# Sixteen loads of the experts' first weights: issued by GpSimd in place of SyncE

## The chip, the cores and the metric

The kernel runs on one core of a Trainium2 chip. The metric is the device time of one launch in microseconds (us), as the median of several runs. A profiled execution gives the trace: which instruction ran on which engine and when, and when each DMA was issued and landed. The engines are TensorE (PE; its weight loads are shown as PEld), VectorE (DVE), ScalarE (ACT), GpSimd (POOL) and SyncE (SP), which here does nothing but issue DMAs. The DMAs of a core run on 16 DMA engines.

## The reference

Three stages follow each other: a causal attention with a window of 64 positions, a soft mixture of experts, and a feed-forward layer with a sigmoid-approximated GELU. All arrays are float32.

```
scores = q @ k.T / sqrt(64), masked to 0 <= i - j < 64    # B, H, S, D = 4, 8, 576, 64
x = softmax(scores) @ v                                   # laid out as 2304 tokens x 512
logits = x @ phi                                          # 512 x 32: 8 experts, 4 slots each
slot_in = softmax over tokens(logits).T @ x
for e in range(8):
    slot_out[e] = relu(slot_in[e] @ w1[e]) @ w2[e]        # w1[e] 512 x 1024, w2[e] 1024 x 512
x = softmax over slots(logits) @ slot_out
h = x @ w_in                                              # 512 x 2048
out = (h * sigmoid(1.702 * h)) @ w_out                    # 2048 x 512
```

w1 and w2 are 16.8 MB each, the largest inputs by far. On the host both are cut into 16 slices of 1 MiB, `[128, 2048]` float32, so that a slice is one DMA with 8 KB for each of the 128 partitions.

## The kernel before

The kernel is one long program with an order written out by hand (`manual_schedule`). Three stages can be told apart in time.

**Attention, with routing in between.** A loop over `i` in 0 to 17 (lines 613 to 672) works on 16 units (a batch and a pair of heads) and two tails. In iteration `i` TensorE computes the scores of unit `i` (`emit_s`, the mask product at L313 and the products at L328), transposes the weights of unit `i - 1` (L348) and multiplies them by v (`emit_pv`, L363). GpSimd prepares what TensorE reads: `scale_q` of the next unit (L236), after that unit's q and k have landed; `set_ones` (L244) and `shift_v` (L248, L251) of this unit, after its v has landed. Every second iteration it also limits a slice of the feed-forward weights that is converted early (`narrow_c`, L161). These are plain Pool instructions, in program order.

SP's order within an iteration is: `load_qk` three units ahead (L226; L228 for the tails), `load_v` two units ahead (L240), and `load_w` (L146), which takes the next slices from the list `plan`: first the 16 of w1, then the 16 of w2. Iterations 2 to 11, 13 and 14 load one slice, 15 and 16 two each, 17 three (`W_AT`, line 35; iteration 12 loads none). For `i` in `AHEAD` (10 to 15) the slice stands between `load_qk` and `load_v`. So w1 is exhausted after iteration 16, and all later calls of `load_w` load w2. `load_qk` waits for its ring of three buffers (the scores of unit `i` have been computed), and `load_v` for its own (the products with v of unit `i - 1`). The slots of w1 are new memory, but for the last three, which held early raw weights.

The first seven slices of w2 go into memory of the attention stage (`dslot`), and are issued as that comes free near the end of the loop and in the tail after it (L691, L720, L745). The last nine go into slots of w1, and are issued as the products with w1 (L792) have read them.

**Experts.** TensorE multiplies by w1 (L792), the result is transposed (`emit_ht`), and it multiplies by w2 (L834; the last slice, in three pieces, at L901).

**Feed-forward.** From there to the end TensorE runs the feed-forward products (L1014, L1046) while SP loads the rest of w_in and w_out.

The line that is changed is in `load_w`:

```
for c in PIECES if not plan else (slice(0, 4),):
    nc.sync.dma_start(out=t[:, c], in_=v[:, c])
```

Of the kernel before, what the change touches and what calls it, by code (L numbers as in the profile page):

```python
# [69 lines left out]
def attention_softmoe_ffn(  # L70
# [12 lines left out]
    nc = tc.nc  # L83
# [41 lines left out]
    def wslot(dtype=F32):  # L125
        return wp.tile([128, 4, 512], dtype, tag="w", name="w")

    def dslot(i):
        return mem(2048 * i, 2048).rearrange("p (a f) -> p a f", a=4)
# [6 lines left out]
    def load_w(n=1):  # L136
        for _ in range(n):
            if plan:
                lst, src, i, d = plan.pop()
                t = wslot() if d is None else dslot(d)  # L140
                v = src[i].rearrange("p (a f) -> p a f", a=4)
                if not plan:
                    t, v = [x.rearrange("p a f -> p (a f)").rearrange(
                        "p (c a f) -> p c a f", c=4, a=4) for x in (t, v)]
                for c in PIECES if not plan else (slice(0, 4),):
                    nc.sync.dma_start(out=t[:, c], in_=v[:, c])  # L146
                lst.append(t)


# [463 lines left out]
    for i in range(ns):  # L613
# [49 lines left out]
        if i in AHEAD:  # L663
            load_w(W_AT.get(i, 0))
# [6 lines left out]
        if i not in AHEAD:  # L671
            load_w(W_AT.get(i, 0))
# [10 lines left out]
        out=ml[:, 128:160], in_=pm[0:1, 0:128].rearrange("p (t s) -> p s t", t=TM), axis=AX.X,  # L683
# [5 lines left out]
    emit_pv(ns - 1)  # L689
    emit_norm(ns - 1)  # L690
    load_w(1)  # L691

    lpt = bank("s")[:, 0:256]
    mm = sp.tile([128, 3], F32, tag="mm", name="mm")

    def tail_logits(t):
# [11 lines left out]
        out=mm[:, 2:3], in0=pm[:, 0:1], scalar1=-1.0, scalar2=None, op0=ALU.mult)  # L708
# [15 lines left out]
        out=ltt, in_=lpt, func=ACTF.Exp, bias=m, scale=1.0, accum_out=ss)  # L724
# [14 lines left out]
    for c in range(2):  # L739
# [9 lines left out]
        out=rsl, in0=pm[:, 0:1], scalar1=ss, scalar2=1e-9, op0=ALU.add, op1=ALU.add)  # L749
# [3 lines left out]
        out=i4s, in0=i4m[:, 0:NS], scalar1=rsl, scalar2=None, op0=ALU.mult)  # L753
    nc.vector.scalar_tensor_tensor(
        out=acc, in0=psl, scalar=al, in1=acc, op0=ALU.mult, op1=ALU.add)
# [479 lines left out]
```

## Time and profile before

| | us |
|---|---|
| runs before, median of 3 | 364.0 (362.63 to 367.21) |
| the profiled execution's own time | 362.31 |
| its span, first to last instruction | 360.5 |
| around the span | 1.8 |

A row of the page's second part cuts the span into 40 slices of 9.0 us, and a digit is the busy share in tenths. In a timeline a row is: start, duration, engine, line, operation, what it writes and reads, and in brackets how long the engine was idle before and what ended that. `SPq` and `POOLq` are the sequencers. An issue of a DMA by SP is short; its landing is told separately. In the chain of waits each row is start, duration and what held the program up. The names: `w` are the slots of 1 MiB, `arena` and `rawt` memory of the attention stage, `in_w_dram` both w1 and w2 in HBM, `in_qk_dram`, `in_vt_dram` and `in_sq_dram` the attention's inputs.

### The profile page before, as it was taken

Reading aid. Unit: us, or ns where it says so; the run is one execution under the profiler, and the core shown is the slowest. Engines: PE = TensorE matmul, PEld = TensorE weight load, DVE = VectorE, ACT = ScalarE, POOL = GpSimd, SP = SyncE. Lnnn points to the kernel's source line nnn. Section 1 sums busy time; section 2 is a strip of 40 time slices with the busy share of each in tenths; the row PEclk is TensorE's granted clock in tenths of the full one; section 3 lists DMA queues with packets and bytes.
Section 4 is the critical chain, followed back from the end, with each engine's and each line's share of the span. In section 5 each row is a group of like instructions: output and inputs, shape, how many; then the busy total and the mean of one; then the engine's idle time right before and its main releaser. Section 6 shows DMA issues by size and latency. Waiting matters only on the chain.

```text
span 360.5 us, 7741 instructions
## 1 busy us (share of the span) xinstructions
PE 351.4 (97%) x3021; PEld 269.9 (75%) x3021; DVE 240.5 (67%) x527; ACT 195.6 (54%) x499; POOL 45.5 (13%) x90
## 2 busy tenths in 40 slices
PE   7999999998999999999999999999999999999995
PEld 6787787776634357888788887788886888888884
DVE  4666797976626228885867695988687876262624
ACT  2898899777314026765657444554455453333330
POOL 4366764630100000000000000000000000000000
PEclk9999999999999999999999999999999999999999
DMA  7999999999999994233131313140300000040404
GB/s 278 407 414 405 409 407 413 402 404 407 418 418 422 418 402 150 101 121 113 60 116 58 119 57 119 32 137 9 116 2 0 0 2 1 0 176 0 175 2 175
DMA packets 18180, 70.87 MB, mean 197 GB/s; under 512 B 2016, under 2 KB 2400, under 8 KB 14176
## 3 DMA queue, kind: packets, MB, share of 16 engines
q1 hardware_dynamic: 18000, 70.18, 50.3%
q8 instruction: 24, 0.39, 0.4%
q10 hardware_dynamic: 144, 0.20, 0.2%
q14 instruction: 12, 0.10, 0.1%
HBM read 65.65 MB, written 4.72 MB: 195 GB/s over the span
## 4 chain that ended last, share of the span: by engine, by line
PE 86%; DMA 9%; ACT 2%; issue 1%; DVE 1%; DVEq 0%; ACTq 0%
PE s L1046 18%; PE t L1046 18%; PE v L1046 18%; DMA w<-in_w_dram 8%; PE v L363 5%; PE m L1014 5%; PE m L348 5%; PE s L328 4%; PE s L313 2%; PE m L401 2%; ACT pa L340 2%; PE m L442 1%; PE m L492 1%; DMA rawt<-in_qk_dram 1%; PE m L928 1%
## 5 line engine op out<-in xcount | busy, mean ns | idle before, releaser
L1002 ACT ACTIVATE r<-m 128x384 fp32r<-128x384 f32 (+1 forms) x97 | 47.4, 491 | 80.6 <-PE m L1014 80.5
L1027 DVE TENSOR_TENSOR r<-g,r 128x384 fp32r<-128x384 f32 x96 | 51.4, 554 | 48.4 <-ACT g L1002 40.0
L1046 PE MATMUL t<-w,r 128*128 128x512 f32 x288 | 75.8, 395 | 0.0
L1046 PE MATMUL s<-w,r 128*128 128x512 f32 x288 | 74.3, 392 | 0.0
L1046 PE MATMUL v<-w,r 128*128 128x512 f32 (+2 forms) x291 | 73.4, 387 | 0.0
L1046 PEld LDWEIGHTS t<-w,r 128*128 128x128 f32 x288 | 53.8, 188 | 14.8 <-issue 4.0
L1046 PEld LDWEIGHTS v<-w,r 128*128 128x128 f32 x291 | 54.5, 188 | 11.3
L1046 PEld LDWEIGHTS s<-w,r 128*128 128x128 f32 x288 | 52.6, 188 | 8.5
L1002 ACT ACTIVATE g<-m 128x384 f32<-128x384 f32 x96 | 47.8, 499 | 0.0
L340 ACT ACTIVATE pa<-s,nm 128x128 f32<-128x128 f32 x140 | 41.0, 404 | 5.6 <-DVE nm L333 5.6
L333 DVE TENSOR_REDUCE nm<-s 128x4 f32<-128x512 f32 x35 | 22.5, 684 | 5.5 <-PE s L328 4.8
L1014 PE MATMUL m<-cT,w 128*128 128x384 f32 (+2 forms) x113 | 25.9, 320 | 0.0
L1014 PEld LDWEIGHTS m<-cT,w 128*128 128x128 f32 x113 | 20.8, 188 | 4.9 <-ACT g L1002 0.7
L348 PE MATMUL m<-ident,pa 128*128 128x128 f32 x144 | 20.9, 283 | 0.8 <-ACT pa L340 0.4
L348 PEld LDWEIGHTS m<-ident,pa 128*128 128x128 f32 x144 | 15.6, 140 | 5.0 <-PE s L328 1.7
L349 ACT COPY pa<-m 128x512 f32<-128x512 f32 x18 | 10.7, 596 | 10.2 <-PE m L348 10.2
L982 ACT CAST w<-wf 128x512 fp32r<-128x512 f32 x15 | 9.3, 623 | 9.3 <-DVE wf L176 9.3
L792 PE MATMUL s<-w,phis 128*32 128x512 f32 x128 | 14.1, 594 | 0.0
L382 DVE TENSOR_TENSOR arena<-v,rs 128x256 f32<-128x256 f32 x36 | 13.6, 420 | 0.6
L328 PE MATMUL s<-arena 64*64 64x128 f32 x352 | 13.8, 271 | 0.1
L985 DVE TENSOR_TENSOR w<-wf,w 128x512 fp32r<-128x512 f32 x15 | 10.3, 689 | 5.2 <-ACT w L982 4.9
L1066 DVE TENSOR_TENSOR w<-s,w 128x512 f32<-128x512 f32 x18 | 11.6, 684 | 2.8 <-PE s L1046 2.8
(218 smaller groups left out, 453.3 us busy)
## 6 DMA issues: line engine op xcount, KB each, us to landing
w<-in_w_dram SPq DMA_DIRECT2D x24, 1024.0 KB, 9.9
w<-in_w_out_dram SPq DMA_DIRECT2D x16, 512.0 KB, 3.4
arena<-in_w_dram SPq DMA_DIRECT2D x7, 1024.0 KB, 11.4
iraw<-in_w_in_dram SPq DMA_DIRECT2D x12, 512.0 KB, 3.3
arena<-in_qk_dram SPq DMA_DIRECT2D x10, 512.0 KB, 8.8
out_dram<-w SPq DMA_DIRECT2D x16, 256.0 KB, 2.1
arena<-in_vt_dram SPq DMA_DIRECT2D x13, 258.5 KB, 7.3
rawt<-in_qk_dram SPq DMA_DIRECT2D x6, 512.0 KB, 8.7
```

What stands on the lines that cost most here:

```text
L328: nc.tensor.matmul(st[h][rows[j], c, :], q, k, start=False, stop=(c == 3), tile_position=(64 * h, 64 * j))
L333: nc.vector.tensor_reduce(out=nm[:, h], in_=st[h], axis=AX.X, op=ALU.max, negate=True)
L340: nc.scalar.activation(out=pb[h][:, c, :], in_=st[h][:, c, :], func=ACTF.Exp, bias=nm[:, h, c:c + 1], scale=1.0)
L348: nc.tensor.transpose(tt[:, c, :], pb[h][:, c, :], ident)
L363: nc.tensor.matmul(pvt[i][h][64 * j:64 * j + 64, c, :], ab[h][:, c, 64 * j:64 * j + 64], v, start=True, stop=True, tile_position=(0, 64 * j))
L382: nc.vector.tensor_tensor(out=o, in0=pv[h][:, :, 1 - h:65 - h], in1=rs[:, h].unsqueeze(2).to_broadcast([128, 4, 64]), op=ALU.mult)
L792: nc.tensor.matmul(ph[32 * j:32 * j + 32, :], siT[:, kk, :], w1t[4 * r + kk][:, j, :], start=(kk == 0), stop=(kk == KD - 1), tile_position ...
L1002: nc.scalar.activation(out=(gh, g)[part][:, a:e], in_=ph[:, a:e], func=ACTF.Gelu_apprx_sigmoid)
L1014: nc.tensor.matmul(ph[:, c - a:e - a], mst[:, f * 128:f * 128 + 128], cT(c, e - c), start=True, stop=True)
L1027: nc.vector.tensor_tensor(out=gl, in0=g, in1=gh.bitcast(F32), op=ALU.subtract)
L1046: nc.tensor.matmul(accs[t][:, h], a[:, c], b[:, h], start=(first and k == 0), stop=(last and k == 2 and h.stop == 512))
L1066: nc.vector.tensor_tensor(out=o[:, h], in0=accs[t][:, h], in1=o[:, h], op=ALU.add)
```

## The change

The 16 loads of w1 slices are issued by GpSimd's queue, and everything else as before by SP. The place of the call in the program is the same, so that a load stands in GpSimd's order behind what GpSimd does earlier in that iteration, and in front of what it does next.

```diff
@@ load_w
                 for c in PIECES if not plan else (slice(0, 4),):
-                    nc.sync.dma_start(out=t[:, c], in_=v[:, c])
+                    (nc.gpsimd if src is w1 else nc.sync).dma_start(out=t[:, c], in_=v[:, c])
                 lst.append(t)
```

## Rows read from the trace of the kernel before

**Rows 1.** The page, parts 1 and 2: busy time; DMA share and rate by slice.
```profile
PE 351.4 (97%) x3021; PEld 269.9 (75%) x3021; DVE 240.5 (67%) x527; ACT 195.6 (54%) x499; POOL 45.5 (13%) x90
...
DMA  7999999999999994233131313140300000040404
GB/s 278 407 414 405 409 407 413 402 404 407 418 418 422 418 402 150 101 121 113 60 116 58 119 57 119 32 137 9 116 2 0 0 2 1 0 176 0 175 2 175
```

**Rows 2.** Busy time of each engine by stretch, clock, DMA share and rate.
```profile
core 0: us, PE busy (x) PEld busy (x) DVE busy (x) ACT busy (x) POOL busy (x), PEclk, DMA share, GB/s
16.00:82.00 66.00, 65.37 (x1272) 51.73 (x1272) 52.56 (x149) 56.99 (x178) 36.12 (x63) 1.00 1.02 407
82.00:131.00 49.00, 46.88 (x515) 23.38 (x507) 22.60 (x67) 15.96 (x41) 2.05 (x3) 1.00 1.01 415
131.00:356.00 225.00, 224.88 (x1041) 183.34 (x1034) 156.11 (x286) 113.76 (x257) 0.00 (x0) 1.00 0.22 76
```

**Rows 3.** The chain that ended last, in order of time, up to 136 us.
```profile
0.74 3.32 DMA rawt<-in_qk_dram
...
99.58 2.76 PE s L792 x24
...
102.35 13.34 DMA w<-in_w_dram
...
115.71 15.08 DMA w<-in_w_dram
...
130.84 0.43 PE v L901 x8
```

**Rows 4.** The page, part 6: DMA issues, KB each, us from issue to landing.
```profile
w<-in_w_dram SPq DMA_DIRECT2D x24, 1024.0 KB, 9.9
...
arena<-in_qk_dram SPq DMA_DIRECT2D x10, 512.0 KB, 8.8
...
arena<-in_vt_dram SPq DMA_DIRECT2D x13, 258.5 KB, 7.3
```

**Rows 5.** Line 146 from 16 to 81.5 us, the loads of w1.
```profile
L146 SPq DMA_DIRECT2D w<-in_w_dram x16: 371/424/1372, 16.3 to 81.4; - x16
...
DMA to landing us min/median/max: 7.3/9.2/10.9
```

**Rows 6.** Timeline of SP, one iteration of the attention loop.
```profile
23.85 0.33 SPq L240 DMA_DIRECT2D rawt<-in_vt_dram  x1
24.23 0.42 SPq L146 DMA_DIRECT2D w<-in_w_dram  x1
25.43 0.33 SPq L226 DMA_DIRECT2D arena<-in_qk_dram  x1
```

**Rows 7.** Timeline of POOL.
```profile
18.61 0.62 POOL L236 TENSOR_SCALAR arena<-arena 128x512 f32<-128x512 f32 x1 [2.53 <-PE m L401]
...
23.30 0.53 POOL L251 TENSOR_SCALAR arena<-arena 64x387 f32<-64x387 f32 x1
23.91 1.92 POOL L161 TENSOR_SCALAR wi<-wi 128x512 f32<-128x512 f32 x1
26.34 0.62 POOL L236 TENSOR_SCALAR rawt<-rawt 128x512 f32<-128x512 f32 x1 [0.51 <-PE m L348]
...
79.51 0.41 POOL L236 TENSOR_SCALAR rawt<-rawt 128x256 f32<-128x256 f32 x1 [2.98 <-DMA rawt<-in_sq_dram]
```

**Rows 8.** Timeline of PE: the score products that read the scaled q.
```profile
20.06 1.17 PE L328 MATMUL s<-arena 64*64 64x128 f32 x32
...
28.31 1.51 PE L328 MATMUL s<-rawt 64*64 64x128 f32 x32
...
80.93 0.29 PE L328 MATMUL s<-rawt 64*64 64x128 f32 x1
```

**Rows 9.** Line 146, the one load of w2 issued at 95.0 us.
```profile
L146 SPq DMA_DIRECT2D arena<-in_w_dram x1: 327/327/327, 95.0 to 95.0; - x1
...
DMA to landing us min/median/max: 8.3/8.3/8.3
```

## The prediction

> **What bounds the kernel now.** I read the page's rate by slice first. From the second slice to the fifteenth, from 9 to 135 us, the 16 DMA engines are busy in every tenth and move 402 to 422 GB/s; from the sixteenth on the rate drops to 150 GB/s and less [rows 1]. By stretch the DMA share is 1.02 from 16 to 82 us and 1.01 from 82 to 131, and 0.22 after that, where PE is busy for 224.88 of 225 us [rows 2]. The reader is to see two programs in one: a first part that takes as long as its bytes take, and a second that takes as long as its matmuls take. The chain of waits agrees. At 102.35 it leaves the products with w1 and stands in two DMAs, of 13.34 and 15.08 us, until PE goes on at 130.84 with the last slice of w2 [rows 3]. So the question for this change is a single one: does the last slice of w2 land earlier or later than 130.8 us? What happens to PE, POOL or the landing of a particular w1 slice before that counts only as far as it makes the DMA engines idle or slow.
>
> In this first part PE is busy too (65.37 of 66 us from 16 to 82 [rows 2]), so attention and transfers run neck and neck. A load waits 7 to 10 us from its issue to its landing [rows 4, 5], while 1 MiB takes 1.05 MB / 415 GB/s = 2.5 us to move. The rest is queue: what was issued earlier moves first. This queue is the cover for everything below.
>
> **The change part by part.** *Bytes.* The same 16 MiB move in either case, and they are issued before w2. At an unbroken rate the last slice lands at 130.8: 0.
>
> *The issues leave SP.* SP issues 16 loads fewer, of 0.42 us each in the median and 1.37 at most [rows 5], 6.8 us in all. SP is no bound: in one iteration it issues at 23.85, 24.23 and 25.43, for 0.3 to 0.4 us each, and waits for buffers between [rows 6]. Its next issue is released by PE, not by the end of the w1 issue. Gain 0. The w2 loads behind it are released by PE or a freed slot as before.
>
> *The issues go to POOL.* No row here shows a DMA that POOL issues. From below it is SP's median of 0.42 us; from above the longest single instruction of POOL in the loop, 1.92 us [rows 5, 7]. I take 1.4, the longest of SP's own issues of this very load, since it is the nearest row. POOL is busy for 36.12 of the 66 us from 16 to 82 [rows 2], so it has 29.9 us idle, 1.87 for each of 16 loads. At 1.4, and even at 1.92 (16 x 0.05 = 0.8 us over), they fit into idle time, which lies mostly where POOL waits for a landing (2.53 and 2.98 us in front of a scaling [rows 7]). What waits behind the load on POOL is the next `scale_q`, and behind that PE's scores. Cost 0; without that cover 16 x 1.4 = 22 us would go onto POOL. The Trainium skill gives a price for such an issue: in "DMA: Bandwidth & Descriptors", section "Latency and other measured facts", a first byte after about 1 us for a DMA from GpSimd against 0.6 us for the other issuers. By it 16 us would be added to POOL, again under 29.9, and the sum stays.
>
> *When the loads are issued.* In the iteration shown SP issues its slice at 24.23 [rows 6]; POOL would reach it after `shift_v` ends at 23.83 and `narrow_c` at 25.83 [rows 7], some 1.6 us later, under the queue of 7 to 10 us. Cost 0.
>
> *Two queues where there was one.* Today a slice of w1 moves behind all q, k and v issued before it. From its own queue it may pass them. From rows 4, an iteration's q and k, v and w1 are 512, 258.5 and 1024 KB. About two slices of w1 were issued but had not landed at any time (9.2 us of latency [rows 5] over iterations of 4.2 to 4.7 us), and at most these two, 5.1 us of transfer, can come in front of a q that stood before them. PE has less cover than that: the scaling that ends at 19.23 is read at 20.06, the one that ends at 26.96 at 28.31, the one that ends at 79.92 at 80.93 [rows 7, 8], so 0.8 to 1.4 us. PE can therefore slip by 0 to 5.1 - 0.8 = 4.3 us. It slips once and not in each iteration, since bytes that came early are not moved again.
>
> *What a slip costs.* Only the loads of w2 are issued in PE's tow. The tightest is that of 95.0 us, which lands at 103.3 [rows 9]: 2.5 us of its own, so the engines have other work until 100.8, 5.8 us after the issue. A transfer that finds the engines free still needs some 2.0 us beside its bytes (the first load takes 3.32 us, of which 0.52 MB at 415 GB/s are 1.3 [rows 3]). So a slip of up to 3.8 us is free, and each us beyond it ends the first part a us later. A slip of 0 to 4.3 costs 0 to 0.5 us. I take 0.5.
>
> *The rate.* Slices of attention move 402 to 414 GB/s, those of w2 alone 418 to 422 [rows 1]. Whether two queues move more or less than one no row tells. Bounds are the best and the worst slice, over the 66 us at 407 GB/s [rows 2]: 66 x (1 - 407/422) = 2.3 us gained, 66 x (407/402 - 1) = 0.8 lost. I take 0, the queue's kind changing no byte.
>
> The sum is +0.5 us on the profiled execution, 362.31 to 362.8. That execution stands 1.7 us under the median of the runs, 364.0, so the forecast in terms of that median is 364.0 + 0.5 = **364.5 us**. A measurement of this kernel can tell about 2%, 7.3 us, from no change; the forecast is no change.
>
> **The rivals.** *w1 passes further than I think.* If POOL's queue gets the larger part of the DMA engines whenever it holds something, q, k and v come late in each iteration, and at the end of attention four slices of w1 (two in iteration 15, two in 16) can stand in front of the last small tails. That would be 10.1 us in front of q's that have 0.8 to 1.4 of cover. POOL itself limits it: a slice is issued only after the q of the next unit and the v of this one have landed. If three slices pass, the slip is 7.6 - 0.8 = 6.8, of which 3.8 are free: +3.0, 367.0. For it speaks that a row of w1 is 8 KB and one of q 4 KB. The Trainium skill says in "DMA: Bandwidth & Descriptors", section "Queues, rings and completion order", that a DMA engine takes turns between queues packet by packet; no row of one queue can show that, and by it larger rows would win the larger part. Against it: total work in the queue is unchanged.
>
> *POOL is held by each load.* This is the rival on the other side. If an issue on POOL takes more than the idle 1.87 us, POOL is the bound of the loop: it slips by 16 x (h - 1.87), of which 3.8 are free, so it decides from h = 2.1 us. At twice the longest issue of SP, 2.7 us, the slip is 13.3 and the loss 9.5: 373.5. For it: POOL's work is serial, `narrow_c` of 1.92 us leaves only 0.51 idle behind it in that iteration [rows 7], and everything that PE reads in the loop goes through POOL. Against it: an issue on SP takes 0.42 and holds nothing up until the landing.
>
> *A better rate.* The small rows of v no longer stand alone in a single queue, and the loop moves at the rate of w2: 364.0 - 2.3 = 361.7. Against it: the engines' share is at 1.02 already.
>
> *The change doesn't do what it says.* If POOL reaches its loads late, because it waits for landings itself, w1 is spread as before and nothing passes anything: 364.0, which the forecast's range holds.
>
> **How the numbers follow.** The forecast, with the last rival's case in it, has 0.72 and a range of its own of 362 to 367 (from a slip that is free on a run 2 us under the median to one with the lost 0.8 of the rate, on runs that spread by 4.6). Passing further has 0.12, POOL held 0.10, a better rate 0.06. The range of 361.5 to 369.5 reaches to the better rate and over the 367.0 of passing further (four slices: 10.1 - 0.8 - 3.8 = 5.5, 369.5), and leaves out the case of a held POOL. Faster by over 7.3 us would take bytes off the first part or a rate of some 435 GB/s over it (410 x 131 / 123.7), which no slice shows: 0.02. Slower by over 7.3 us is POOL held, less a part of it where h is just over 2.1, with a little for what I don't know of this queue: 0.10. Within 2%: 0.88.
>
> **What would show it.** Right, if the DMA share stays at 1.0 from 9 to 131 us, POOL shows 16 new rows at line 146 of under 2 us each, its busy time rises by some 22 us, SP's line 146 is left with the 18 issues of w2, and the last slice of w2 lands at 130 to 132. The latency of w1 should fall under 9.2 us and that of q and k rise, with PE's waits before L328 or L363 in the loop growing by 0 to 4 us in all. Wrong, if POOL's rows are over 2.1 us and PE waits for POOL in each iteration, if a DMA slice before 131 us shows under 9 tenths, or if the rate from 16 to 82 us leaves 402 to 422 GB/s. After 131 us nothing should differ: PE's 224.88 of 225 us stay as they are.

## The result, and the profile after

| | before | after |
|---|---|---|
| median of 20 runs each, us | 363.3 (362.21 to 369.5) | 366.42 (364.14 to 369.62) |
| the profiled execution, us | 362.31 | 368.38 |
| its span, us | 360.5 | 366.6 |

The ratio of after to before is 1.0069 (1.0042 to 1.0096), which is 363.3 x 0.0069 = 2.5 us (1.5 to 3.5): slower, surely, and by less than the 2% that count as a difference here. It is a ratio of means, without the few slow runs (18 runs of before, 19 of after); the medians stand 3.1 us apart. The profiled execution stands 2.0 us above the median of its kernel, so I also use a second profile of the same kernel, the last of the experiments below, of 365.76 us.

The first view is the page of after, parts 1 and 2 (it answers to [rows 1]).

```profile
PE 354.3 (97%) x3021; PEld 271.7 (74%) x3021; DVE 240.4 (66%) x527; ACT 195.8 (53%) x499; POOL 54.2 (15%) x106
...
PEclk9999999999699999999999999999999999999999
DMA  7999999999999995324021405031300000040404
GB/s 285 408 411 402 388 339 421 354 409 394 420 383 417 418 405 201 114 66 166 20 100 54 156 18 172 2 116 57 114 2 0 0 2 1 0 164 10 172 2 173
```

The rate was 402 to 422 in every slice from 9 to 135 us. Now the fifth, sixth, eighth, tenth and twelfth slices show 388, 339, 354, 394 and 383, although each digit of the share is still a 9, and the sixteenth holds 201 where it held 150: bytes have moved later. PEclk, flat at 9 before, has a 6 in the eleventh slice. POOL has 16 instructions more and 54.2 - 45.5 = 8.7 us.

By stretch, after (columns as in [rows 2]):

```profile
16.00:82.00 66.00, 63.53 (x1229) 50.04 (x1223) 50.65 (x143) 54.62 (x169) 43.19 (x74) 1.00 1.01 389
82.00:100.00 18.00, 15.45 (x212) 12.20 (x208) 10.20 (x40) 9.08 (x30) 1.83 (x7) 0.85 1.02 408
100.00:131.00 31.00, 30.40 (x269) 12.32 (x265) 13.57 (x33) 8.70 (x19) 1.83 (x1) 0.98 0.99 406
...
138.00:356.00 218.00, 217.88 (x1001) 177.51 (x1001) 152.61 (x280) 113.71 (x257) 0.00 (x0) 1.00 0.21 71
```

From 16 to 82 us PE is idle for 2.47 us where it was idle for 0.63, and the rate is 389 GB/s against 407 [rows 2]. Both of the things that bound this part are late, and the rest is untouched.

The chain that ended last in after, its longest pieces up to 136 us (it answers to [rows 3]):

```profile
74.96 8.51 DMA rawt<-in_sq_dram
...
105.87 7.00 PE s L792 x64
113.96 7.00 PE s L792 x64
123.08 12.15 PE v L834 x112
```

The two DMAs of w2 are gone from it. In their place stands the load of the last tail of q, and no DMA after it: from 83.47 to 105.87 us the chain is PE's, with short pieces of the other engines and one pause of 1.98 us at 91.34, and from 105.87 to 136.58 PE alone.

How much PE is late at each point can be worked out from the traces: the start of each PE instruction less the start of the same one in the profiled execution before, as a median over 4 us from the time named (time of before), in us.

| trace | 12 | 28 | 44 | 76 | 88 | 100 | 140 to the end |
|---|---|---|---|---|---|---|---|
| after | -0.01 | 0.97 | 2.02 | 2.29 | 3.49 | 6.30 | 5.95 |
| after, second profile | 0.76 | 1.26 | 1.76 | 1.92 | 3.71 | 3.70 | 3.35 |
| after, third profile | -0.56 | 1.02 | 1.82 | 3.00 | 7.16 | 7.14 | 6.79 |
| loop of before (slack of PE) | 0.44 | 0.46 | 0.52 | 0.80 | 1.34 | | |
| loop of before (other way round) | 0.53 | 0.50 | 0.49 | 0.77 | 1.02 | 1.03 | |

The last two rows are experiments in which nothing differs from before up to 90 us. They show the noise: between 12 and 76 us an unchanged loop gains 0.36 and 0.24 us of lateness, and up to 88 us 0.90 and 0.49. The changed loop loses in three places, near 24 to 28, 36 to 48 and 80 to 88, and what it has lost at 100 stays to the end, but for 0.34 us. The second profile's 3.70 - 0.76 - 0.34 = 2.6 us is close to the measured 2.5. This is one execution: the other two give 6.0 and 7.4 by the same sum, and they took 2.0 and 2.6 us more than the median of after.

### The profile page after: what moved, and what is told of

The parts are those of the page before. It is cut to its first block, busy times and chain, and to the rows that moved or that the text cites. A ratio compares the mean times of both kernels' runs of the same rounds, so it can differ in the third digit from the quotient of the medians.

```text
span 366.6 us, 7759 instructions
## 1 busy us (share of the span) xinstructions
PE 354.3 (97%) x3021; PEld 271.7 (74%) x3021; DVE 240.4 (66%) x527; ACT 195.8 (53%) x499; POOL 54.2 (15%) x106
## 4 chain that ended last, share of the span: by engine, by line
PE 87%; DMA 3%; ACT 3%; DVE 3%; issue 2%; POOL 1%; DVEq 0%; ACTq 0%; POOLq 0%; SPq 0%
PE s L1046 18%; PE t L1046 18%; PE v L1046 18%; PE m L1014 5%; PE s L792 4%; PE v L363 3%; PE s L328 3%; PE v L834 3%; PE m L348 3%; DMA rawt<-in_sq_dram 2%; PE m L401 2%; ACT pa L340 2%; PE s L313 1%; PE m L442 1%; PE m L492 1%
## 5 line engine op out<-in xcount | busy, mean ns | idle before, releaser
L349 ACT COPY pa<-m 128x512 f32<-128x512 f32 x18 | 10.7, 597 | 13.0 <-PE m L348 13.0
L792 PE MATMUL s<-w,phis 128*32 128x512 f32 x128 | 14.1, 594 | 0.0
```

The source lines that it names most:

```text
L792: nc.tensor.matmul(ph[32 * j:32 * j + 32, :], siT[:, kk, :], w1t[4 * r + kk][:, j, :], start=(kk == 0), stop=(kk == KD - 1), tile_position ...
```

## The experiments

Theory A, made from these views: PE has no slack, so each us that PE slips in attention is a us at the end. It slips because single loads of q, k and v land late, when slices of w1 from the second queue move in front of them, which I call passing. The rival B is the prediction's own sum: a slip up to 3.8 us is free, and what costs is the later landing of w2, from a lower rate.

**The change in halves.** First the first 12 slices on GpSimd and the last 4 on SP, then the last 4 alone on GpSimd.

```diff
-(nc.gpsimd if src is w1 else nc.sync).dma_start(out=t[:, c], in_=v[:, c])
+(nc.gpsimd if src is w1 and i < 12 else nc.sync).dma_start(out=t[:, c], in_=v[:, c])    # first
+(nc.gpsimd if src is w1 and i >= 12 else nc.sync).dma_start(out=t[:, c], in_=v[:, c])   # second
```

> The first twelve slices of w1 stay on GpSimd, the last four go back to SP. Theory L (late tails): the loss comes from the last four slices, which pass the last q tail and so stop PE at 75 to 84 us; without them 363.3 to 364.0 us, and PE waits for no in_sq landing over 1 us. Theory K (the two queues together move less over the whole loop, 389 against 407 GB/s): 12 of 16 slices keep three quarters of the loss of 2.5 us, 365.2 us, and the rate from 16 to 82 us stays under 397 GB/s.

> Only the last four slices of w1 are issued by GpSimd. Theory L: nearly the whole loss, 365.5 to 366.5 us, with a wait of POOL for the last in_sq landing of 5 us or more and PE behind it. Theory K: a quarter of the loss, 363.9 us.

Measured: 366.01 us, 1.0074 (1.0041 to 1.0107), and 365.37, 1.0064 (1.0023 to 1.0105). Either half costs nearly what the whole costs (+2.7 and +2.3 us, each known to 1.2 or 1.5 us), so the parts do not seem to add. With the last four on SP the last tail of q lands after 6.86 us, close to the 6.43 of before, the rate from 16 to 82 us is 397 GB/s, and PE is late by 1.68 at 100 us. With only the last four on GpSimd the same tail lands after 6.22 us, so the late tail that was expected of that half is not there. The windows of that second half show where it changes:

```profile
16.00:40.00 24.00, 23.69 (x480) 19.43 (x480) 16.84 (x46) 21.24 (x66) 14.21 (x24) 1.00 1.03 408
40.00:60.00 20.00, 20.00 (x389) 16.11 (x380) 17.25 (x51) 18.06 (x57) 11.98 (x19) 1.00 1.02 410
60.00:82.00 22.00, 21.54 (x414) 16.19 (x416) 17.85 (x54) 17.36 (x57) 12.75 (x25) 1.00 0.95 368
```

The last columns, clock, DMA share and GB/s, are those of before up to 60 us (408 and 409 there). Then four slices that come late from GpSimd leave the DMA engines 5% idle and the rate at 368, where before had 404 at a share of 1.02. Here w2 ends last: its last piece lands at 132.24 instead of 130.79. Both profiled executions (364.94 and 364.40 us) are about 1 us under the median of their kernel, so the rows show ways of losing, not the whole sizes: PE's slip in the first half, a lower rate in the second. PE ends 1.3 and 1.4 us late in them; the rest of what they took longer than before, 1.3 and 0.6 us, stands behind the last product, where the kernels are the same.

**Another engine's queue.** All 16 slices issued by ScalarE.

```diff
-(nc.gpsimd if src is w1 else nc.sync).dma_start(out=t[:, c], in_=v[:, c])
+(nc.scalar if src is w1 else nc.sync).dma_start(out=t[:, c], in_=v[:, c])
```

> All 16 slices issued by ScalarE, a second queue like SP's own, at the same places. If any second queue lets w1 pass the attention's loads, the loss stays: 365.5 to 366.5 us, w1 lands sooner than SP's q and the rate from 16 to 82 us falls under 397 GB/s. If it is GpSimd's queue in particular, 363.3 to 364.0 us. A third way, that the issue itself holds ScalarE (95% busy in parts of the loop), would give over 368 us with 0.4 us or more in each row of ScalarE's issue.

Measured: 367.63, 1.0111 (1.006 to 1.0161). No better. From 16 to 82 us it moves 369 GB/s at a share of 0.98, and PE waits for one scaling of q for 2.9 us, a scaling that itself waits 6.29 us for its q to land. ScalarE's issues take 0.33 us each, under the 0.4 that were to be the sign of a held ScalarE. So the harm doesn't need GpSimd's queue; a second queue from ScalarE does it too.

**The slack of PE.** The kernel before, with 32 unused products ahead of the experts' first ones. This adds work that the kernel does not need.

```diff
+    warm(32)
     emit_w1(0)
```

> The kernel before, with 32 additional products of 128x128 on PE (unused, into a bank of their own) between the end of attention and the first product with w1: PE is 4.1 us later there by 32 x 0.128 us. Theory A: PE's own work from there to the last slice of w2 fills the stretch but for some 0.9 us, so the end moves by 3.2 us, 366.5 us. Theory B, that of the prediction: 3.8 us of a slip are free, so 363.3 to 363.6 us.

Measured: 370.04, 1.0167 (1.0116 to 1.0218), which is +6.1 us (4.2 to 7.9). PE in this run, where the added products are line 779:

```profile
103.13 0.63 PE L766 MATMUL m<-i4s,acc 128*128 128x32 f32 x4 [0.30 <-ACT phis L768]
103.60 7.39 PE L779 MATMUL v<-ident 128*128 128x128 f32 x64
110.92 7.07 PE L792 MATMUL s<-w,phis 128*32 128x512 f32 x64
```

The 32 products are 64 rows and delay PE by 7.2 us (L792 starts 7.79 after the last L766 row, and 0.57 in before), more than I had meant. With no slack but 0.34 us that makes +6.9; with 3.8 us free it makes +3.4, which lies outside the interval of 4.2 to 7.9. The profiled execution says the same: PE was 4.2 us late ahead of the products (a granted clock of 0.81 from 82 to 100 us) and 11.4 behind them, and it took 373.37 - 362.31 = 11.1 us longer. So PE has no slack, and this half of A holds. That loads land late by passing is the other half, which this run doesn't touch.

**Smaller rows.** After, with each slice as two DMAs of 4 KB rows.

```diff
-for c in PIECES if not plan else (slice(0, 4),):
+for c in PIECES if not plan else (slice(0, 2), slice(2, 4)) if src is w1 else (slice(0, 4),):
```

> As the changed kernel, but each slice of w1 goes as two DMAs of 4 KB rows from GpSimd, the row size of q and k. If w1 passes q and v because its row is twice as large at each turn, its part of the engines falls from 2/3 to 1/2 against q: q and v land sooner, PE slips under 2 us up to 84 us, and the time falls by a third to a half of the loss, to about 364.8 to 365.3 us. If rows don't matter, 366.0 to 366.4 us as the change; GpSimd then has 32 issues of some 0.6 us, 9 us more, which fit into its idle time.

Measured: 367.21, 1.0103 (1.0066 to 1.014), no gain. In the profiled execution, which at 370.43 us is 3.2 above its median, the rate from 16 to 82 us is 368 and PE is 8.24 us late at 100. That the size of w1's rows sets the harm is not borne out. It is not a clean test, since GpSimd now spends 1.1 us on each slice.

**The other way round.** w1 on SP, and the last nine slices of w2 on GpSimd, so that attention has one queue and the experts' stage two.

```diff
-(nc.gpsimd if src is w1 else nc.sync).dma_start(out=t[:, c], in_=v[:, c])
+(nc.gpsimd if src is w2 and i >= 7 else nc.sync).dma_start(out=t[:, c], in_=v[:, c])
```

> The kernel before, w1 from SP, but the last nine slices of w2 (11 DMAs) from GpSimd. There is little else on SP's queue at that time (six feed-forward slices behind them). If GpSimd's queue itself moves less, the rate from 110 to 130 us falls under 412 GB/s against 415, and the last slice lands over 1 us later, 364.5 us or more. If it moves as much as SP's and the loss comes only from what passes what, 362.8 to 363.6 us, provided the feed-forward slices don't pass w2: if they do (6 x 0.5 MB, 7.6 us at most), the last slice lands by as much later as what passes, 366 us or more, with w_out slices landing before the last w2.

Measured: 371.9, 1.0221 (1.0149 to 1.0293). The attention loop is that of before (406 GB/s from 16 to 82 us, PE 1.03 late at 100), and from 100 to 131 us the rate is even 417, so a queue of GpSimd loses nothing by itself. The DMA view from 114 to 131 us, where both queues have work all the time, by queue (packets, MB, share of the 16 engines; q0 is GpSimd's, q1 is SP's), and PE's waits:

```profile
q0 software_dynamic: 639, 4.66, 66.4%
q1 hardware_dynamic: 642, 2.37, 34.5%
```

```profile
131.82 1.06 PE L834 MATMUL v<-w,rawt 128*32 128x512 f32 x8 [2.70 <-DMA w<-in_w_dram]
135.69 1.51 PE L893 MATMUL m<-w,rawt 128*32 128x256 f32 x16 [2.81 <-DMA w<-in_w_dram]
```

The two queues moved 639 and 642 packets: they take turns. The turn is a single packet, here one row: of the rows that start within 5 ns before the end of another, 1193 belong to the other queue and 122 to the same. SP's are the feed-forward weights, which stood behind w2 in one queue and now move beside it. Slices of w2 land 3.77 us apart (124.24, 128.01, 131.78) where 2.5 had been enough, two thirds of the rate, as 8 KB against 4 KB in turn would make it. PE waits twice, and the last piece lands at 139.11. Here passing is shown at its plainest. The Trainium skill says in "DMA: Bandwidth & Descriptors", section "Queues, rings and completion order", that a DMA engine goes round its queues a packet at a time. The trace agrees, with its 639 and 642 packets.

**Later and earlier.** First each slice of after one iteration later, then each slice in front of GpSimd's own work of its iteration.

```diff
-W_AT = {**{i: 1 for i in range(2, 17)}, 12: 0, 15: 2, 16: 2, 17: 3}    # first
+W_AT = {**{i: 1 for i in range(3, 16)}, 13: 0, 16: 2, 17: 5}
@@ second: ahead of scale_q, set_ones and shift_v
+        if i <= NU:
+            load_w(W_AT.get(i, 0))
         if 1 < i < NU - 1:
             scale_q(i + 1, nc.gpsimd)
...
-        if i in AHEAD:
-            load_w(W_AT.get(i, 0))
...
-        if i not in AHEAD:
+        if i > NU:
             load_w(W_AT.get(i, 0))
```

> As the changed kernel, but each slice of w1 stands one iteration later, so that the q, k and v which it passed have mostly landed. If passing is the cause, q lands within 8 to 9 us as before, PE slips under 1 us up to 84 us and the time is 363.2 to 364.2 us, unless the engines now run dry (DMA share under 0.99 from 16 to 82 us). If it is the two queues as such, the rate from 16 to 82 us stays under 397 GB/s and the time at 366 us.

> As the changed kernel, but within an iteration each slice of w1 stands in front of GpSimd's scaling, ones and shift, so that it doesn't wait for the landings of that iteration's q and v. In the changed kernel it was issued 2.5 to 6.7 us after SP's time for it. Theory late (the queue gets thinner and engines run dry): issued at SP's times or before, the rate from 16 to 82 us is back over 402 GB/s, and the last slice of w2 lands by 131.5 us, while PE still slips by 2 us or more, since w1 passes q and v as much or more: 365 to 366.5 us. Theory two queues (engines get out of step whenever two queues are served): the rate stays under 397 GB/s. If passing and being late together are the whole loss, and POOL's place cures neither, 366 us or more.

Measured: 367.98, 1.0105 (1.0049 to 1.016), and 369.39, 1.0149 (1.0043 to 1.0256). The later one, its window of the loop and PE at the end of w2:

```profile
16.00:82.00 66.00, 64.40 (x1262) 50.98 (x1257) 51.61 (x146) 55.77 (x174) 42.60 (x77) 1.00 0.97 375
```

```profile
130.75 1.07 PE L834 MATMUL v<-w,rawt 128*32 128x512 f32 x8 [1.22 <-DMA w<-in_w_dram]
...
133.37 1.51 PE L893 MATMUL m<-w,rawt 128*32 128x256 f32 x16 [1.55 <-DMA w<-in_w_dram]
```

The earlier one, two windows:

```profile
16.00:82.00 66.00, 60.41 (x1161) 47.17 (x1155) 48.32 (x135) 52.63 (x164) 43.23 (x74) 1.00 1.01 401
82.00:100.00 18.00, 15.81 (x282) 13.00 (x279) 11.37 (x40) 11.65 (x37) 1.29 (x7) 1.00 0.94 357
```

They fail at opposite ends. Later, PE is only 1.45 us late at 100, little passes, but the engines have too little to do (share 0.97) and w2 ends last: PE waits for it and is 5.63 late. Earlier, the loop moves 401 GB/s, but PE is 7.29 us late at 100; its w2 loads, issued in its tow, are then late too, and the rate falls to 357. In one queue both are had: the load is issued early and still moves behind the loads that stand before it.

**The change again, twice.** The kernel after, unaltered, with each of the last two groups.

> The changed kernel once more, for a trace at an undisturbed clock: 366 us, PE 3.2 to 3.6 us late at the first product with w1, and the end of the program late by 0.3 us less than that.

> The changed kernel once more, for a trace at an undisturbed clock: about 366 us, PE 3.2 to 3.6 us late at the first product with w1, the last slice of w2 landing at 133 to 135 us.

Measured: 367.78, 1.0102 (1.0012 to 1.0192) of two runs only, and 365.72, 1.0039 (0.9988 to 1.0089). The first result, 1.0069, lies in both intervals. PE is 7.14 us late at the first product with w1 in the first of the two, where 3.2 to 3.6 had been expected, and 3.70 in the second; the last slice of w2 lands at 136.01 and 133.31. Their traces are the second and third profiles of the table above (the second is the run of 365.76 us).

## Why the prediction came out as it did

The time was forecast at +0.5 us and is +2.5, inside the range and within 2%. That it lies inside is owed to a range of 8 us, not to the mechanism: the forecast has the end of the first part set by the bytes of w2, and it was set by PE. Four of its steps were wrong in kind or in size, and one of them decided. By its own test the rate from 16 to 82 us would show it wrong if it left 402 to 422 GB/s, and it did.

**The step that failed: "a slip of up to 3.8 us is free".** It counted only what a slip does to w2's loads, having read from the chain of waits that DMA alone ends the first part. PE in before, its share from 100 to 131 us (columns as in [rows 2]), and then its rows from the end of attention to the last slice of w2:

```profile
100.00:131.00 31.00, 30.77 (x313) 11.27 (x305) 11.33 (x25) 6.03 (x11) 0.00 (x0) 1.00 1.01 415
```

```profile
99.51 7.07 PE L792 MATMUL s<-w,phis 128*32 128x512 f32 x64
...
116.72 6.22 PE L834 MATMUL v<-arena,rawt 128*32 128x512 f32 x56
122.75 6.19 PE L834 MATMUL v<-w,rawt 128*32 128x512 f32 x56
128.76 0.83 PE L893 MATMUL m<-w,rawt 128*32 128x256 f32 x16
...
130.84 0.43 PE L901 MATMUL v<-w,rawt 128*32 128x128 f32 x8 [0.23 <-DMA w<-in_w_dram]
```

PE is busy there for 30.77 of the 31 us from 100 to 131, and the wait that the chain hung 28.4 us of DMA on is one of 0.23 us. The chain names what came last, not by how much. Before was bound by PE and by w2 to within 0.3 us. The same rows after:

```profile
105.80 7.07 PE L792 MATMUL s<-w,phis 128*32 128x512 f32 x64
...
123.01 6.22 PE L834 MATMUL v<-arena,rawt 128*32 128x512 f32 x56
129.04 6.19 PE L834 MATMUL v<-w,rawt 128*32 128x512 f32 x56
...
136.57 0.40 PE L901 MATMUL v<-w,rawt 128*32 128x128 f32 x8
```

They start 6.29 us later, and the rows behind them, from 132 us of before on, 5.95, with no wait for a DMA: the slip went to the end less 0.34. The last slice of w2 landed at 134.85, 4.1 us later than before and 1.7 us before PE wanted it. The delay experiment shows the same slack without a second queue. With 0.34 in place of 3.8, the prediction's own slip of 0 to 4.3 us would have given 0 to 4.0, which holds the measured 2.5.

**"It slips once and not in each iteration": wrong.** Two queues do pass each other, as the step said, and the sum of PE's slip, 3.70 - 0.76 = 2.9 us in the second profile, is within its 4.3. In the other two profiles it is 6.3, of which 2.0 are the clock's (below), and 7.7, past the bound. And PE slips in three places. The clearest is the last. By queue, from the issue of the last tail of q to its landing, first after (74.96 to 83.47 us), then before (72.9 to 79.4):

```profile
q0 software_dynamic: 379, 2.74, 77.9%
q1 hardware_dynamic: 320, 0.72, 22.3%
```

```profile
q1 hardware_dynamic: 574, 2.59, 100.2%
```

After, SP's queue needed only 0.72 MB, of which the tail is 0.39, but GpSimd's took 2.74 MB meanwhile, in packets that are 2.74 / 379 = 7.2 KB on average to SP's 2.3. The tail landed after 8.51, 9.79 and 11.51 us in the three traces, and after 6.43, 5.98 and 5.91 in the three with the loop of before. What it costs shows on POOL, in after and in its second profile (it answers to the last row of [rows 7]):

```profile
75.80 1.11 POOL L146 DMA_DIRECT2D w<-in_w_dram  x2
76.98 0.40 POOL L236 TENSOR_SCALAR arena<-arena 128x256 f32<-128x256 f32 x1
83.61 0.41 POOL L236 TENSOR_SCALAR rawt<-rawt 128x256 f32<-128x256 f32 x1 [6.24 <-DMA rawt<-in_sq_dram]
```

```profile
84.80 0.41 POOL L236 TENSOR_SCALAR rawt<-rawt 128x256 f32<-128x256 f32 x1 [8.31 <-DMA rawt<-in_sq_dram]
```

And on PE, again in after and in its second profile:

```profile
84.07 0.32 PE L328 MATMUL s<-rawt 64*64 64x128 f32 x1 [0.58 <-POOL arena L244]
```

```profile
85.25 0.32 PE L328 MATMUL s<-rawt 64*64 64x128 f32 x1 [2.13 <-POOL arena L244]
```

POOL waits 6.24 and 8.31 us where it waited 2.98, and PE's scores, at 80.93 before [rows 8], start at 84.07 and 85.25, behind waits of 0.58 and 2.13 us (3.30 in the third profile). Not every load suffers: the mean latency of q and k from 12 to 82 us is 9.16 before, 9.52 after and 9.09 in the second profile, with extremes of 8.2 and 11.1, 4.7 and 11.7, and 5.6 and 11.0. It is single loads that are late, and PE gets nothing for one that is early. The first place is like the last: the two q loads issued near 14 and 18 us land after 10.2 to 11.4 and 10.7 to 12.1 us in the three profiles, and after 7.7 to 8.2 and 8.5 to 9.0 in the three with the loop of before. In after PE waits 0.72 us at 25.11 for the scaling behind the first of them, where before it waits for none. That the slip of the middle place, some 0.5 us in the second profile and so near the noise, has the same cause is argued.

**"Some 1.6 us later, under the queue: cost 0": the size was wrong.** POOL in after, two iterations:

```profile
38.90 0.59 POOL L146 DMA_DIRECT2D w<-in_w_dram  x1
40.97 0.61 POOL L236 TENSOR_SCALAR rawt<-rawt 128x512 f32<-128x512 f32 x1 [1.48 <-DMA rawt<-in_qk_dram]
44.07 0.11 POOL L244 MEMSET arena<- 128x5 f32 x1 [2.49 <-DMA arena<-in_vt_dram]
...
45.45 1.92 POOL L161 TENSOR_SCALAR wi<-wi 128x512 f32<-128x512 f32 x1
47.32 0.59 POOL L146 DMA_DIRECT2D w<-in_w_dram  x1
```

SP issued the slice of the last row at 43.70 in before. GpSimd comes to it at 47.32, behind a wait for a v that is itself late (it landed after 9.38 us) and behind `narrow_c`. The eleventh slice went at 63.39 and goes at 70.08, 6.7 us later, since in iterations 10 to 15 SP's load stood ahead of its v and GpSimd's stands behind. I had taken the delay from one iteration, a mild one. Then the queue runs thin: from 48 to 52 us after shows 340 GB/s at a share of 0.92, and from 68 to 72 it shows 316 at 0.93, where before has 414 and 404.

**"The rate: 0", bounds 2.3 gained to 0.8 lost: outside its bounds.** 389 GB/s over 66 us is 66 x (1 - 389/407) = 2.9 us of bytes. It did not set the end in after, since PE was later still; it did where only the last four slices moved and where all moved one iteration later.

**Right.** GpSimd's issue takes 0.53 to 0.72 us, between the bounds of 0.42 and 1.92 and under the 1.4 taken, and its 8.7 us fit into idle time but for 0.2 us: in the second and third profiles PE waits 0.24 and 0.21 us near 30 us for a scaling whose q has landed at 28.64 and 28.75, but which POOL starts at 29.31 and 29.08, behind an issue of 0.63 us. The rival that POOL is held is refuted at its size, which wanted issues of over 2.1 us. POOL's busy time, by the same token, did not rise by the 22 us named as a sign. SP gained nothing, as said. After 131 us nothing differs: PE's lateness is 5.93 to 5.96 from 132 us to the last instruction, and it is busy for 217.88 of 218 us. Of the rivals, "w1 passes further" named the mechanism and came near the time (367.0), but by luck: its sum takes the same 3.8 us as free. A better rate did not come, and 16 issues on POOL refute that the change doesn't do what it says.

**The clock is not the cause, but adds to it.** The profiled execution of after had a stretch with a granted clock at the lower of its two levels, 1.2 GHz: from 96 to 100 us its row says 0.50, after PE had stood idle for 1.98 us at 91.34. In the second profile it fell from 82 to 89 us (0.81), around PE's wait of 2.13 us for the tail. The price by rows of the chain, after and then its second profile:

```profile
94.01 1.47 PE s L699 x8
...
97.25 1.90 PE s L699 x8
99.15 1.87 PE m L492 x8
```

```profile
94.18 1.09 PE s L699 x8
...
96.46 1.16 PE s L699 x8
97.61 1.00 PE m L492 x8
```

These three groups take 5.24 us against 3.25, 2.0 more, which is as much as the execution stands above its median. Yet the runs whose mean clock was 0.998 or more have medians of 362.95 (35 runs of before, from the experiments) and 366.14 (9 of the 20 of after). That is 3.2 us, as far apart as the medians of all runs. So the clock is not what makes the difference.

**Open.** Why a thin second queue lets the 16 DMA engines drift apart (below) isn't settled: only that ScalarE's queue does it too. Nor is it settled why the last four slices alone cost 2.3 us in the runs, of which their one trace shows 1.4. Every version with two queues that was run is slower than the kernel before, and none was found that beats it.

## What to carry to other kernels

One queue is also an order: a large load issued early in the same queue moves behind the small ones that stand before it, and loses that place when it gets a queue of its own. Before calling a slip free, look at the other engine over the same stretch: a chain of waits that stands in a DMA for 28 us may hang on a wait of 0.2, and an engine busy for 30.77 of 31 us has next to no slack. And a load that is moved to another engine is issued when that engine's own waits let it, in its worst iteration and not in the one you looked at.

## What the hardware showed that I had not expected

- An issue of 1 MiB of w1 by GpSimd holds it for 0.59 us in the median (0.53 for the slices of w2 in the other-way-round run), against 0.42 on SP and 0.33 on ScalarE.
- The 16 engines can drift further apart under two queues. The first and the last of the 16 completion counts of one DMA lie up to 7.5 us apart in after (a q load issued at 35.84 us, 39.91 to 47.42), 6.8 in its second profile and 5.1 with ScalarE's queue, against 3.2 before and 3.8 in the delay experiment, which has before's loop. The last tail of q is no such load: its counts lie 3.5 us apart in after, 2.3 in the second profile and 3.1 before. In the median of the loads from 12 to 82 us the distance hardly changes (1.95 before, 2.18 in the delay experiment, 2.35 after, 2.14 in the second profile), so it is single loads that are drawn apart. How much of the loss is owed to this is not shown.
- Two queues with work took equal numbers of packets, 639 and 642 in 17 us, although one moved 4.66 MB with them and the other 2.37.
- In all three traces of the changed kernel the granted clock fell at or after PE's longest wait (2.0, 2.1 and 3.3 us, shares of 0.50, 0.81 and 0.67 in the stretch with the lowest).
